# A weight conversion inside a mixture-of-experts kernel: its square one call later, its calls spread over the experts in another way

## The chip, the cores and the metric

The kernel runs on one core of a Trainium2 chip. Its time is device time in microseconds (us) of one execution; several runs are given by their median. A profile is one further execution, recorded by the hardware. Engines are called PE (TensorE, matmuls), DVE (VectorE), ACT (ScalarE), POOL (GpSimd) and SP (SyncE, which issues most DMAs).

## What is computed

Attention over 2304 tokens gives x (512 wide). Each token goes to two of eight experts, and a dense layer follows; the last two steps are

```python
top2 = np.argpartition(-noisy_logits, 2, axis=1)[:, :2]
h = np.maximum(x[mask] @ w1[e], 0.0)                  # 512 -> 1024, per expert e
out[mask] += top2_w[mask, k, None] * (h @ w2[e])      # 1024 -> 512
h = x @ w_in                                          # 512 -> 2048
g = np.maximum(0.01 * h, h)
return (g @ w_out).astype(np.float32)                 # 2048 -> 512
```

`w_in` and `w_out` come from random numbers divided by a square root, so they are 64-bit floats. The kernel gets their raw bits and turns them into 32-bit floats itself.

## The kernel before

**Stages.** Attention and routing come first, then the eight experts, then the dense layer. An expert has 640 rows of tokens (5 blocks of 128). A float32 matmul is made of three: every operand is kept as a rounded "high" half, written by ACT, and a "low" half (the difference, written by DVE).

**One expert.** `hidden(e, f)` (PE line 742) runs for f = 0 to 7: 24 matmuls into the PSUM tile ph, of which there are two; ACT writes the high half of hT (line 751), DVE the low half (752). Then, for each block k = 0 to 4: `transposed` turns the next expert's tokens (PE line 215 into the PSUM tile xtp, two of them; ACT 217 and DVE 218 write the halves of xT), and `expert_out(e, k)` runs 24 matmuls (line 763) into the PSUM tile py, two of them; ACT line 773 copies py out as ys, and SP stores that in y_d. `feed` loads weight chunks of later experts and splits them (ACT line 154, DVE 156).

**The conversion.** `narrow()` is the call that the change is about. 64 pieces of 128 x 256 numbers go through it as through a pipeline, one stage each per call. In the call that converts piece j: DVE lines 708, 711, 714 and 715 take the bits apart (715 is the last one that reads the low words), POOL line 718 adds, and ACT line 719 squares the high words into k, which lies in the place of the low words. In the next call, DVE line 689 compares k with a constant, which zeroes numbers that are too small. Pieces 0 to 31 (`w_out`) are then stored. Two pieces of `w_in` make one tile w8: POOL line 700 forms four sums from it, and two later calls split it (ACT line 670, DVE 672) and store it (SP lines 671, 675).

**Order.** In the expert stage ACT and DVE keep the order in which the program is written. The order of PE, POOL and SP is chosen when the kernel is built, by a scheduler with a model of the times; so an edit to ACT and DVE can also move matmuls.

**Where it is called.** In expert 0: 7 calls. In experts 1 to 6: at f = 0, 2, 4 and 6, and once after every block k, 9 calls. In expert 7: at every f, 8 calls. That is 69, as many as the 64 pieces and the stages behind them need. A loop after expert 7 would make up for calls that are missing.

Of the kernel before, what the change touches and what calls it, by code (L numbers as in the profile page):

```python
# [15 lines left out]
AF = mybir.ActivationFunctionType  # L16
# [12 lines left out]
E = 8  # L29
# [27 lines left out]
FH, FK, NF = 2, 2, 2  # L57
# [45 lines left out]
def body(ctx: ExitStack, tc, qT, kT, v, wgc, noise, eye, cst, w1, w2, win, wout, out):  # L103
    nc = tc.nc
# [53 lines left out]
    def feed(n, upto, pool=False):  # L158

        while loading:  # L160
            split_half(pool)
        for _ in range(n):
            if state["next"] < 2 * min(len(chunks), upto):
                c, h = divmod(state["next"], 2)
                state["next"] += 1
                raw = rawp.tile([P, 512], F32, tag="raw", name="raw")
                nc.sync.dma_start(raw, chunks[c][:, h * 512 : (h + 1) * 512])
                loading.append((c, h, raw))
# [33 lines left out]
    def gather(e, k):  # L202
        xg[e, k] = st.tile([P, DM], F32, tag="st", name="xg")
        i = k * E + e
        nc.gpsimd.indirect_dma_start(
            out=xg[e, k],
            out_offset=None,
            in_=x_d[0 : T1 * P if k < K1 else N, :],
            in_offset=bass.IndirectOffsetOnAxis(ap=gidx[:, i : i + 1], axis=0),
        )  # L210

    def transposed(src, dst, k):
        pt = b1.tile([P, 4, P], F32, tag="b1", name="xtp")
        for d in range(4):
            nc.tensor.transpose(pt[:, d, :], src[:, d * P : (d + 1) * P], ident)
        sl = slice(k * P, (k + 1) * P)
        nc.scalar.activation(dst[:, :, 0, sl], pt, AF.Copy)  # L217
        nc.vector.tensor_tensor(
            dst[:, :, 1, sl], pt, dst[:, :, 0, sl].bitcast(F32), op=ALU.subtract
        )  # L220
# [441 lines left out]
    loaded, converting, parted = [], [], []  # L662

    def narrow():

        if parted and parted[0][1] is not None:
            i, part, w8, x = parted[0]
            sl = slice(512 * x, 512 * x + 512)
            hi = cv.tile([P, 512], F32R, tag="hi", name="cvhi", bufs=1)
            nc.scalar.activation(hi, w8[:, sl], AF.Copy)  # L670
            nc.sync.dma_start(combos[i][:, part, 0, sl], hi.bitcast(F32))
            nc.vector.tensor_tensor(
                w8[:, sl].bitcast(F32R), w8[:, sl], hi.bitcast(F32), op=ALU.subtract
            )
            nc.sync.dma_start(combos[i][:, part, 1, sl], w8[:, sl])
            parted[0][3] += 1
            if x:
                parted.pop(0)
        if converting:
            c, part, k, mf = converting.pop(0)  # L680
            if c < 8:
                w = cv.tile([P, CV], F32, tag="w", name="cvw")
            else:
                if part % 2 == 0:
                    w8 = cv.tile([P, 1024], F32, tag="cvq", name="cvq")
                    parted.append([c - 8, None, w8, 0])
                w8 = parted[-1][2]
                w = w8[:, part % 2 * CV : (part % 2 + 1) * CV]
            nc.vector.scalar_tensor_tensor(w, k, SMALL, mf, op0=ALU.is_ge, op1=ALU.mult)
            if c < 8:  # L690
                nc.sync.dma_start(singles[c][:, part * CV : (part + 1) * CV], w)
            elif part % 2:
                q = lambda i: w8[:, i * P : (i + 1) * P]
                for d, x, y, op in (
                    (S1, A21, A22, ALU.add),
                    (S2, S1, A11, ALU.subtract),
                    (S3, A11, A21, ALU.subtract),
                    (S4, A12, S2, ALU.subtract),
                ):
                    nc.gpsimd.tensor_tensor(q(d), q(x), q(y), op=op)  # L700
                parted[-1][1] = part // 2
        if len(loaded) > 1 or loaded and state["narrowed"] == 16 * 1024 // CV:
            c, part, raw = loaded.pop(0)
            low, high = raw[:, :, 0], raw[:, :, 1]
            a = cv.tile([P, CV], I32, tag="a", name="cva", bufs=1)
            m = cv.tile([P, CV], I32, tag="m", name="cvm")
            mf, hf, k = m.bitcast(F32), high.bitcast(F32), low.bitcast(F32)
            nc.vector.tensor_scalar(
                a, high, 3, 0x3FFFFFF8, op0=ALU.logical_shift_left, op1=ALU.bitwise_and
            )  # L710
            nc.vector.scalar_tensor_tensor(
                a, high, -0x40000000, a, op0=ALU.bitwise_and, op1=ALU.bitwise_or
            )
            nc.vector.tensor_single_scalar(m, a, -0x800000, op=ALU.bitwise_and)
            nc.vector.scalar_tensor_tensor(  # L715
                mf, low.bitcast(U32), 2.0**-52, mf, op0=ALU.mult, op1=ALU.mult
            )
            nc.gpsimd.tensor_tensor(mf, mf, a.bitcast(F32), op=ALU.add)  # L718
            nc.scalar.activation(k, hf, AF.Square)  # L719
            converting.append((c, part, k, mf))  # L720
        i = state["narrowed"]
        if i < 16 * 1024 // CV:
            state["narrowed"] += 1
            c, part = divmod(i, 1024 // CV)
            raw = cv.tile([P, CV, 2], I32, tag="raw64", name="raw64", bufs=3)
            words = doubles[c].bitcast(I32).rearrange("p (n t) -> p n t", t=2)
            nc.sync.dma_start(raw, words[:, part * CV : (part + 1) * CV])
            loaded.append((c, part, raw))
# [3 lines left out]
    def hidden(e, f, n0=0, n1=CAP):  # L732

        parts = [(n0, n1)] if n1 - n0 <= 512 else [(0, 320), (320, 640)]
        m = parts[0][1] - parts[0][0]
        w = slot(8 * e + f // 2)
        ps = big.tile([P, 2, 512], F32, tag="big", name="ph")
        for d in range(4):
            col = d * 256 + (f % 2) * P
            for a, b in TERMS:  # L740
                for h, (m0, m1) in enumerate(parts):
                    nc.tensor.matmul(  # L742
                        ps[:, h, 0:m],
                        w[:, a, col : col + P],
                        xT[:, d, b, m0:m1],
                        start=(d == 0 and a == 0 and b == 0),
                        stop=(d == 3 and a == 1),
                    )
        src = ps[:, 0 : len(parts), 0:m]
        hv = hT[:, f, :, n0:n1].rearrange("p s (h n) -> p s h n", n=m)  # L750
        nc.scalar.activation(hv[:, 0], src, AF.Relu)  # L751
        nc.vector.scalar_tensor_tensor(  # L752
            hv[:, 1], src, 0.0, hv[:, 0].bitcast(F32), op0=ALU.max, op1=ALU.subtract
        )
# [22 lines left out]
    def expert_out(e, k):  # L777
        for _ in expert_parts(e, k):
            pass
# [144 lines left out]
    with tc.manual_schedule(engines=ORDERED0):  # L924
# [12 lines left out]
        for k in range(K1):  # L937
            for i, _ in enumerate(expert_parts(0, k)):
# [4 lines left out]
                if k == K1 - 1 and i >= TI and late:  # L943
                    gather_late()
                    e, j = late.pop(0)
# [9 lines left out]
    with tc.manual_schedule(engines=ORDERED):  # L955
        for f in range(8):
            hidden(0, f, K1 * P, CAP)
            feed(FH, (f + 1) // 2 + RING)
            if f % NF == 0:
                narrow()  # L960
            if f >= 8 - NB + K1:
                gather(1, f - 8 + NB)
    with tc.manual_schedule(engines=ORDERED):
        for k in range(NB):
            transposed(xg[1, k], xT, k)
        for k in range(K1, NB):
            expert_out(0, k)
            feed(FK, 4 + RING)
            narrow()
        for e in range(1, E):  # L970
            for f in range(8):
                hidden(e, f)
                feed(FH, 8 * e + (f + 1) // 2 + RING)
                if f % NF == 0 or e + 1 == E:
                    narrow()
                next(tokens, None)
                if f >= 3 and e + 1 < E:
                    gather(e + 1, f - 3)
            if e + 1 == E:
                break  # L980
            for k in range(NB):
                transposed(xg[e + 1, k], xT, k)
                expert_out(e, k)
                feed(FK, 8 * e + 4 + RING)
                narrow()
# [392 lines left out]
```

## Time and profile before

| | |
|---|---|
| median of 3 runs | 1010.89 us (1010.03 to 1013.91) |
| the profiled execution | 1014.06 us, its span 1012.3 us |
| PE busy | 960.9 us (95%), weight loads 862.7 us (85%) |
| DVE, ACT, POOL busy | 645.4 us, 376.1 us, 228.2 us |
| experts 1 to 7 | from about 186 us to about 607 us of the span |
| first and last of the 64 squares (line 719) | 174.9 us and 582.3 us |

Busy time is the time in which an engine executes. The view of the waits lists, for each pair of instructions, how long an engine sat idle in front of the first one, and which instruction ended that.

### The profile page before, as it was taken

The page shows a single profiled execution, that of the slowest core. Times are in us where ns is not written, and L with a number is a line of the kernel's source. Part 1 is how long each engine was busy: PE and PEld are TensorE (multiplying, and loading weights), DVE is VectorE, ACT ScalarE, POOL GpSimd, SP SyncE. Part 2 cuts the span into 40 slices and gives each one's busy share as a digit, 9 for nine tenths or more (in the row PEclk, how much of TensorE's full clock was granted, in tenths as well). Part 3 has the DMA queues.
Part 4 walks back from the last instruction along what each step waited for, and adds up shares of the span by engine and source line. Part 5 has one row for each costly group of instructions (what it writes and reads, how often), then busy time and mean ns, then how long its engine had stood idle before and what let it go on. Part 6 is the DMA issues. An engine that isn't in the chain of part 4 may idle for free. (4 is left out here: it accounts for less than half of the span.)

```text
span 1012.3 us, 15783 instructions
## 1 busy us (share of the span) xinstructions
PE 960.9 (95%) x5782; PEld 862.7 (85%) x5782; DVE 645.4 (64%) x1354; ACT 376.1 (37%) x729; POOL 228.2 (23%) x325
## 2 busy tenths in 40 slices
PE   6889879999999999999999998999999999999998
PEld 4788768998989899797897977989989988998897
DVE  5688855686775657766767833475566566556553
ACT  2644424443443434345353443332242232324112
POOL 2873452203122131422313222101001100000000
PEclk7889879999999999999999999999999999999999
DMA  9941346656465564866667586765646645645541
GB/s 267 323 156 62 101 143 194 219 175 210 147 192 164 187 185 157 264 202 222 213 207 224 201 285 229 257 247 207 230 171 210 244 168 200 222 148 193 213 146 42
DMA packets 85906, 198.09 MB, mean 196 GB/s; under 512 B 8960, under 2 KB 14528, under 8 KB 84672
## 3 DMA queue, kind: packets, MB, share of 16 engines
q1 hardware_dynamic: 79744, 177.11, 51.9%
q0 software_dynamic: 6080, 19.93, 6.5%
q8 instruction: 46, 0.75, 0.3%
q14 instruction: 36, 0.29, 0.1%
HBM read 156.11 MB, written 40.89 MB: 195 GB/s over the span
## 5 line engine op out<-in xcount | busy, mean ns | idle before, releaser
L1280 PE MATMUL po<-whB,gT 128*128 128x512 f32 x864 | 203.9, 392 | 0.0
L1280 PEld LDWEIGHTS po<-whB,gT 128*128 128x128 f32 x864 | 159.8, 188 | 31.9
L1244 PEld LDWEIGHTS pp<-zB,whA 128*128 128x128 f32 x1344 | 165.4, 192 | 6.9 <-ACT tmp L1252 3.5
L1244 PE MATMUL pp<-zB,whA 128*128 128x256 f32 x1344 | 167.7, 283 | 3.1 <-ACT tmp L1252 2.7
L763 PE MATMUL py<-whB,hT 128*128 128x512 f32 x600 | 148.8, 395 | 2.5 <-ACT ys L773 2.1
L742 PE MATMUL ph<-xT,whB 128*128 128x320 f32 x960 | 146.9, 309 | 2.4 <-ACT xT L217 2.4
L742 PEld LDWEIGHTS ph<-xT,whB 128*128 128x128 f32 x960 | 143.1, 188 | 5.8 <-ACT xT L217 3.1
L763 PEld LDWEIGHTS py<-whB,hT 128*128 128x128 f32 x600 | 109.6, 188 | 24.7 <-ACT ys L773 3.6
L1225 DVE TENSOR_TENSOR tmp<-tmp,pp 128x256 f32<-128x256 f32 x160 | 65.2, 418 | 65.5 <-PE pp L1244 61.6
L752 DVE SCALAR_TENSOR_TENSOR hT<-ph,hT 128x640 fp32r<-128x640 f32 (+2 forms) x72 | 53.9, 749 | 77.2 <-ACT hT L751 77.1
L742 PE MATMUL ph<-xT,whA 128*128 128x320 f32 (+2 forms) x576 | 94.2, 322 | 6.3 <-DVE hT L752 3.8
L742 PEld LDWEIGHTS ph<-xT,whA 128*128 128x128 f32 x576 | 90.2, 200 | 9.2 <-DVE hT L752 4.0
L763 PE MATMUL py<-whA,hT 128*128 128x512 f32 x360 | 89.3, 395 | 3.7 <-ACT ys L773 2.7
L1233 ACT ACTIVATE gT<-tmp 128x512 fp32r<-128x512 f32 x64 | 40.5, 632 | 134.5 <-DVE tmp L1230 134.5
L719 ACT ACTIVATE raw<-raw 128x256 f32<-128x256 f32 x64 | 28.1, 438 | 163.9 <-DVE cvm L715 132.7
L895 POOL DMA_INDIRECT g<-y_d,rows x36 | 34.0, 945 | 242.3 <-DVE g L906 167.8
L763 PEld LDWEIGHTS py<-whA,hT 128*128 128x128 f32 x360 | 65.6, 188 | 18.8 <-ACT ys L773 4.3
L718 POOL TENSOR_TENSOR cvm<-cvm,cva 128x256 f32<-128x256 f32 x64 | 48.0, 750 | 138.0 <-DVE cvm L715 120.8
L1234 DVE TENSOR_TENSOR gT<-tmp,gT 128x512 fp32r<-128x512 f32 x64 | 44.3, 692 | 46.3 <-ACT gT L1233 46.3
L751 ACT ACTIVATE hT<-ph 128x640 fp32r<-128x640 f32 (+2 forms) x72 | 45.9, 638 | 64.6 <-PE ph L742 64.6
L156 DVE TENSOR_TENSOR whB<-raw,whB 128x512 fp32r<-128x512 f32 x89 | 58.7, 688 | 10.5 <-ACT whB L154 10.3
L154 ACT ACTIVATE whB<-raw 128x512 fp32r<-128x512 f32 x96 | 57.2, 624 | 12.7 <-DMA raw<-in_w 8.3
(192 smaller groups left out, 1144.8 us busy)
## 6 DMA issues: line engine op xcount, KB each, us to landing
whA<-ws SPq DMA_DIRECT2D x64, 896.0 KB
raw<-in_w SPq DMA_DIRECT2D x128, 256.0 KB
y_d<-ys SPq DMA_DIRECT2D x40, 256.0 KB
raw<-in_wout SPq DMA_DIRECT2D x32, 256.0 KB
raw<-in_win SPq DMA_DIRECT2D x32, 256.0 KB
ws<-cvhi SPq DMA_DIRECT2D x32, 256.0 KB
ws<-cvq SPq DMA_DIRECT2D x32, 256.0 KB
whA<-ws SPq DMA_DIRECT2D x10, 512.0 KB
```

The source lines that it names most:

```text
L154: nc.scalar.activation(s[:, 0, sl], raw, AF.Copy)
L156: eng.tensor_tensor(s[:, 1, sl], raw, s[:, 0, sl].bitcast(F32), op=ALU.subtract)
L718: nc.gpsimd.tensor_tensor(mf, mf, a.bitcast(F32), op=ALU.add)
L742: nc.tensor.matmul(ps[:, h, 0:m], w[:, a, col : col + P], xT[:, d, b, m0:m1], start=(d == 0 and a == 0 and b == 0), stop=(d == 3 and a == 1),)
L751: nc.scalar.activation(hv[:, 0], src, AF.Relu)
L752: nc.vector.scalar_tensor_tensor(hv[:, 1], src, 0.0, hv[:, 0].bitcast(F32), op0=ALU.max, op1=ALU.subtract)
L763: nc.tensor.matmul(ps, hT[:, f, a, sl], w[:, b, col : col + DM], start=(f == 0 and a == 0 and b == 0), stop=(f == 7 and a == 1),)
L1225: add = lambda o, x, y: nc.vector.tensor_tensor(o, x, y, op=ALU.add)
L1233: nc.scalar.activation(gT[:, h, 0], ch(h), AF.Copy)
L1234: nc.vector.tensor_tensor(gT[:, h, 1], ch(h), gT[:, h, 0].bitcast(F32), op=ALU.subtract)
L1244: nc.tensor.matmul(out_, w[:, part, a, q * P : (q + 1) * P], zT["B"][:, j, part, b], start=(part == 0 and a == 0 and b == 0), stop=(part = ...
L1280: nc.tensor.matmul(sums[t], gT[:, h, a, sl], w[:, b, h * DM : (h + 1) * DM], start=(fp + h + a + b == 0), stop=(fp == 7 and h == 1 and a = ...
```

## The change

In `narrow()` the square moves from the call that takes a piece apart to the call after it, in front of the comparison that uses it and behind the split of the tile before. And the calls are spread differently: experts 1 to 6 get one more call, at f = 5 (10 instead of 9), and expert 7 has calls at f = 0, 2, 4 and 6 (4 instead of 8), 71 in all.

```diff
         if converting:
-            c, part, k, mf = converting.pop(0)
+            c, part, k, hf, mf = converting.pop(0)
+            nc.scalar.activation(k, hf, AF.Square)
             if c < 8:
...
             nc.gpsimd.tensor_tensor(mf, mf, a.bitcast(F32), op=ALU.add)
-            nc.scalar.activation(k, hf, AF.Square)
-            converting.append((c, part, k, mf))
+            converting.append((c, part, k, hf, mf))
...
             for f in range(8):
                 hidden(e, f)
                 feed(FH, 8 * e + (f + 1) // 2 + RING)
-                if f % NF == 0 or e + 1 == E:
+                if f % 2 == 0 or f == 5 and e + 1 < E:
                     narrow()
```

Three places show what moves. In the changed kernel the lines of the conversion have numbers one higher (715 is 716, 689 is 690), and the square is line 681.

**First place:** ACT and DVE in expert 5, from one block of tokens (k = 2) to the next. raw64 is a piece's tile of raw words, with the number of the piece's tile. ACT before:

```order
L217 ACTIVATE xT_109<-xtp_4961 128x4x128
L773 ACTIVATE ys_4993<-py_4968 128x512
L670 ACTIVATE cvhi_4996<-cvq_4894 128x512
L719 ACTIVATE raw64_4904<-raw64_4904 128x256
L217 ACTIVATE xT_109<-xtp_5013 128x4x128
```

DVE before, in the same stretch:

```order
L218 TENSOR_TENSOR xT_109<-xtp_4961,xT_109 128x4x128
L672 TENSOR_TENSOR cvq_4894<-cvq_4894,cvhi_4996 128x512
L689 SCALAR_TENSOR_TENSOR cvq_5001<-raw64_4809,cvm_4952 128x256
L708 TENSOR_SCALAR cva_5003<-raw64_4904 128x256
L711 SCALAR_TENSOR_TENSOR cva_5003<-raw64_4904,cva_5003 128x256
L714 TENSOR_SCALAR cvm_5004<-cva_5003 128x256
L715 SCALAR_TENSOR_TENSOR cvm_5004<-raw64_4904,cvm_5004 128x256
L218 TENSOR_TENSOR xT_109<-xtp_5013,xT_109 128x4x128
```

ACT's square is on tile 4904, which DVE takes apart in this very stretch; line 715 stands between. ACT in the changed kernel:

```order
L217 ACTIVATE xT_109<-xtp_5051 128x4x128
L773 ACTIVATE ys_5083<-py_5058 128x512
L670 ACTIVATE cvhi_5086<-cvq_4890 128x512
L681 ACTIVATE raw64_4899<-raw64_4899 128x256
L217 ACTIVATE xT_109<-xtp_5106 128x4x128
```

DVE in the changed kernel, in the same stretch:

```order
L218 TENSOR_TENSOR xT_109<-xtp_5051,xT_109 128x4x128
L672 TENSOR_TENSOR cvq_4890<-cvq_4890,cvhi_5086 128x512
L690 SCALAR_TENSOR_TENSOR cvq_5040<-raw64_4899,cvm_5043 128x256
L709 TENSOR_SCALAR cva_5097<-raw64_4997 128x256
L712 SCALAR_TENSOR_TENSOR cva_5097<-raw64_4997,cva_5097 128x256
L715 TENSOR_SCALAR cvm_5098<-cva_5097 128x256
L716 SCALAR_TENSOR_TENSOR cvm_5098<-raw64_4997,cvm_5098 128x256
L218 TENSOR_TENSOR xT_109<-xtp_5106,xT_109 128x4x128
```

The square is now on the tile that was taken apart a call earlier (4899), and DVE compares that tile (line 690) right behind it; the piece that DVE now takes apart (4997) is squared in the next call.

**Second place:** PE from the end of expert 5's hidden layer to the start of expert 6's. Of the groups of transposes (line 215) the last in each list is expert 7's, the others are expert 6's blocks 2 to 4. Before:

```order
L742 MATMUL ph<-xT,whB 128x320 x24
L763 MATMUL py<-whB,hT 128x512 x16
L215 MATMUL xtp<-ident,xg 128x128 x4
L763 MATMUL py<-whB,hT 128x512 x43
L215 MATMUL xtp<-ident,xg 128x128 x4
L763 MATMUL py<-whB,hT 128x512 x5
L742 MATMUL ph<-xT,whA 128x320 x2
L763 MATMUL py<-whB,hT 128x512 x13
L215 MATMUL xtp<-ident,xg 128x128 x4
L763 MATMUL py<-whB,hT 128x512 x11
L215 MATMUL xtp<-ident,xg 128x128 x4
L742 MATMUL ph<-xT,whA 128x320 x46
```

and in the changed kernel:

```order
L742 MATMUL ph<-xT,whB 128x320 x48
L763 MATMUL py<-whB,hT 128x512 x9
L742 MATMUL ph<-xT,whB 128x320 x24
L763 MATMUL py<-whB,hT 128x512 x23
L215 MATMUL xtp<-ident,xg 128x128 x4
L763 MATMUL py<-whB,hT 128x512 x41
L215 MATMUL xtp<-ident,xg 128x128 x4
L763 MATMUL py<-whB,hT 128x512 x11
L215 MATMUL xtp<-ident,xg 128x128 x4
L763 MATMUL py<-whB,hT 128x512 x20
L742 MATMUL ph<-xT,whA 128x320 x6
L215 MATMUL xtp<-ident,xg 128x128 x4
L742 MATMUL ph<-xT,whA 128x320 x42
```

The transpose of expert 6's last block, which had 11 matmuls of line 763 behind it before the hidden layer went on, now has 20. Behind f = 7, the last 24 matmuls of line 742, stand 23 of line 763 instead of 16.

**Third place:** PE from expert 0 to expert 1. Before:

```order
L763 MATMUL py<-whB,hT 128x512 x8
L742 MATMUL ph<-xT,whB 128x320
L215 MATMUL xtp<-ident,xg 128x128 x4
L763 MATMUL py<-whB,hT 128x512 x4
L215 MATMUL xtp<-ident,xg 128x128 x4
L763 MATMUL py<-whB,hT 128x512 x2
L742 MATMUL ph<-xT,whB 128x320 x23
L763 MATMUL py<-whB,hT 128x512 x24
```

and in the changed kernel:

```order
L763 MATMUL py<-whB,hT 128x512 x15
L742 MATMUL ph<-xT,whB 128x320 x2
L215 MATMUL xtp<-ident,xg 128x128 x8
L742 MATMUL ph<-xT,whB 128x320 x4
L763 MATMUL py<-whB,hT 128x512 x24
L742 MATMUL ph<-xT,whB 128x320 x42
```

The last transpose of expert 1's tokens had six matmuls of line 763 and another transpose behind it; now it has the transpose alone, and the matmuls that need its result follow at once.

## Rows read from the trace of the kernel before

**Rows 1.** The page's head and its busy times: engine, us, share of span, instructions.

```profile
span 1012.3 us, 15783 instructions
PE 960.9 (95%) x5782; PEld 862.7 (85%) x5782; DVE 645.4 (64%) x1354; ACT 376.1 (37%) x729; POOL 228.2 (23%) x325
```

**Rows 2.** Stretches: from:to, length, busy us (instructions) per engine, PE clock, DMA share, GB/s.

```profile
300.00:400.00 100.00, 99.98 (x589) 91.91 (x588) 60.39 (x124) 39.26 (x73) 22.22 (x28) 1.00 0.54 171
400.00:500.00 100.00, 94.96 (x525) 83.36 (x524) 70.72 (x138) 43.48 (x84) 35.34 (x56) 1.00 0.70 232
500.00:600.00 100.00, 94.66 (x528) 83.87 (x528) 71.20 (x133) 45.78 (x87) 24.40 (x42) 1.00 0.65 213
```

**Rows 3.** Waits, 170 to 600 us: who for whom, us in total, times, longest.

```profile
ACT raw L719 <- DVE cvm L715: 132.7, 48, 3.4
...
ACT whA L154 <- DMA raw<-in_w: 6.7, 7, 2.5
...
PE py L763 <- ACT ys L773: 4.8, 6, 1.6
...
PE ph L742 <- ACT xT L217: 3.7, 3, 1.4
...
PE py L763 <- ACT hT L751: 1.4, 3, 0.5
PE xtp L215 <- DVE xT L218: 1.3, 2, 1.0
```

**Rows 4.** PE in time, expert 5 to 6: start, us, instruction, count, [idle before].

```profile
484.52 0.60 PE L215 MATMUL xtp<-ident,xg 128*128 128x128 f32 x4
...
489.41 2.90 PE L742 MATMUL ph<-xT,whA 128*128 128x320 f32 x17 [1.33 <-ACT xT L217]
```

**Rows 5.** ACT in time, the same stretch.

```profile
484.25 0.59 ACT L773 ACTIVATE ys<-py 128x512 f32<-128x512 f32 x1
484.72 0.64 ACT L670 ACTIVATE cvhi<-cvq 128x512 fp32r<-128x512 f32 x1
488.44 0.43 ACT L719 ACTIVATE raw<-raw 128x256 f32<-128x256 f32 x1 [3.09 <-DVE cvm L715]
488.78 0.58 ACT L217 ACTIVATE xT<-xtp 128x512 fp32r<-128x512 f32 x1
```

**Rows 6.** DVE in time, the same stretch.

```profile
485.39 0.72 DVE L672 TENSOR_TENSOR cvq<-cvq,cvhi 128x512 fp32r<-128x512 f32 x1 [0.31 <-ACT cvhi L670]
...
487.78 0.63 DVE L715 SCALAR_TENSOR_TENSOR cvm<-raw,cvm 128x256 f32<-128x256 uint32 x1
489.39 0.69 DVE L218 TENSOR_TENSOR xT<-xtp,xT 128x512 fp32r<-128x512 f32 x1 [0.98 <-ACT xT L217]
```

**Rows 7.** DVE in time, hidden layer of expert 7, two calls in a row.

```profile
559.95 0.82 DVE L752 SCALAR_TENSOR_TENSOR hT<-ph,hT 128x640 fp32r<-128x640 f32 x1 [1.09 <-ACT hT L751]
...
564.24 0.64 DVE L715 SCALAR_TENSOR_TENSOR cvm<-raw,cvm 128x256 f32<-128x256 uint32 x1
565.97 0.82 DVE L752 SCALAR_TENSOR_TENSOR hT<-ph,hT 128x640 fp32r<-128x640 f32 x1 [1.09 <-ACT hT L751]
...
570.12 0.43 DVE L715 SCALAR_TENSOR_TENSOR cvm<-raw,cvm 128x256 f32<-128x256 uint32 x1
```

**Rows 8.** PE in time, hidden layer and outputs of expert 7.

```profile
558.33 3.68 PE L742 MATMUL ph<-xT,whB 128*128 128x320 f32 x24
...
593.16 14.39 PE L763 MATMUL py<-whA,hT 128*128 128x512 f32 x62 [1.62 <-ACT ys L773]
```

**Rows 9.** POOL in time, hidden layer of expert 7.

```profile
562.99 1.60 POOL L700 TENSOR_TENSOR cvq<-cvq 128x128 f32<-128x128 f32 x3 [3.31 <-DVE cvq L689]
564.96 0.74 POOL L718 TENSOR_TENSOR cvm<-cvm,cva 128x256 f32<-128x256 f32 x1 [0.36 <-DVE cvm L715]
```

**Rows 10.** ACT and DVE in time, expert 0 to expert 1.

```profile
184.69 0.62 ACT L217 ACTIVATE xT<-xtp 128x512 fp32r<-128x512 f32 x1
...
185.54 0.68 DVE L218 TENSOR_TENSOR xT<-xtp,xT 128x512 fp32r<-128x512 f32 x1
```

## The prediction

> **What bounds the kernel now.** The head of the page and its busy times come first: a span of 1012.3 us of which PE is busy 960.9 us [rows 1]. A gain must come out of the 51 us in which PE stands still, unless PE's work itself changes, and here it does not. The view by stretches then says where the change can act. The first piece is squared at 174.9 us and the last at 582.3 us, so experts 1 to 7 are the place. From 300 to 400 us PE is busy for 99.98 of 100 us, from 400 to 500 for 94.96 and from 500 to 600 for 94.66 [rows 2]. PE's clock is 1.00 in all three. So 5.0 + 5.3 = 10.4 us of idle PE lie where the pieces of `w_in` are split and stored besides being converted.
>
> The view of the waits from 170 to 600 us names who ends that idle time. PE waits 14 times: 4.8 us for ys, 3.7 for the high half of xT, 1.4 for hT, 1.3 for the low half of xT, 11.2 us together [rows 3]. All but the last are ACT's, and far above them in that view stands ACT itself: 132.7 us, 48 times, in front of the square (line 719), until DVE's line 715 is done [rows 3]. That costs nothing by itself, since ACT has time to spare. It costs something where PE wants an ACT instruction that stands behind the square.
>
> The three engines in order of time, at the start of expert 6, show one such case. PE transposes the last block at 484.52 us [rows 4]. ACT could copy it at once; but it has begun the split at 484.72, then waits 3.09 us for line 715, squares at 488.44, and copies the block at 488.78 [rows 5]. DVE ends line 715 at 487.78 + 0.63 = 488.41, writes the low half at 489.39 [rows 6], and PE's hidden layer starts at 489.41 after 1.33 us of waiting [rows 4]. The other waits that I followed, in experts 5 and 7, have the same pattern: a square just ahead on ACT, or DVE behind an ACT that was held up. The longest, 1.62 us, is in expert 7 [rows 8].
>
> **The change, part by part.** *The square a call later.* Its operand has then been ready for a whole call, so ACT no longer waits in front of it. Removed from PE's path: up to 11.2 us [rows 3]. The square still takes its 0.43 us of ACT [rows 5], 64 times, beside PE's work, as before.
>
> *The wait that is added.* DVE's comparison (690) now needs a square that stands behind ys and the split on the same ACT. Queued behind it on DVE are the four steps on the next piece and the low half of the next block, for which PE waits. From the start of ys to the end of that low half: ys to split 484.72 - 484.25 = 0.47 us, split to its subtraction 485.39 - 484.72 = 0.67 [rows 5, 6], from there to the end of line 715 488.41 - 485.39 = 3.02, the low half 0.69 [rows 6]; together 4.85 us. The square, 0.43 us, runs beside the subtraction of 0.72, so it adds nothing. ys of block 3 starts when PE has ended that block, and PE has the 24 matmuls of block 4 before the hidden layer of the next expert. At 14.39 us for 62 [rows 8] these take 5.57 us. That covers 4.85 with 0.7 to spare; so I charge only 0.3 us at each of the four expert changes 3-4 to 6-7, the size of DVE's wait for the split today (0.31) [rows 6]: **1.2 us**. Bounds: 0, and 4 x 1.33 = 5.3 us if every change waits as today [rows 4].
>
> *PE's new order.* At the change to expert 6 the last transpose has 20 matmuls behind it instead of 11, so the block has 9 x 0.23 = 2.1 us more to arrive: that is what makes the 4.85 us above fit. At expert 0 to 1 it is the other way round. The matmuls that need the last block now follow one transpose (0.60 us [rows 4]) behind it, and the copies take 0.62 on ACT and 0.68 on DVE [rows 10]: 1.30 - 0.60 = **0.7 us** lost. Bounds: 0 if the copies start early, 1.3 if nothing overlaps.
>
> *One call more in experts 1 to 6, four fewer in expert 7.* The work of the 64 pieces is the same. A call with everything that DVE does for one f lasts 559.95 to 564.88 us, 4.93 us, or 565.97 to 570.55, 4.58 us [rows 7]. In the new order PE has, from the end of f = 4 to the end of f = 7, three times 24 matmuls of 3.68 us [rows 8] and 14 of line 763: 14.3 us. DVE, now with calls at f = 4, 5 and 6, needs 3 x 4.93 = 14.8 us at most. What is late by 0.5 us is covered by the matmuls behind f = 7, 23 of line 763, of which 6 at most need f = 7: 17 x 0.23 = 3.9 us. Cost 0; if that cover were gone, 0.5 us x 6 = 3 us. The extra call also issues two stores and a load on SP and adds to POOL (three sums are 1.60 us, the addition 0.74 [rows 9]); neither is waited for by PE directly, and both are idle most of the time (POOL 228 of 1012 us [rows 1]). In expert 7 the calls vanish from f = 1, 3, 5 and 7, and with them what held up its share of the 11.2 us; nothing is counted twice.
>
> **Sum:** -11.2 + 1.2 + 0.7 = -9.3 us. The profiled execution took 1014.06 us, so it would take 1004.8. It lies 3.2 us above the median of the three runs, 1010.89; from the median the same sum gives **1001.6 us**.
>
> The Trainium skill, Perfetto Trace Analysis, section Identifying the Most-Contended Engine, says that matmul busy time misjudges how near TensorE is to its limit, and that the busy share of weight loads is the better measure. Here weight loads fall from 91.91 us in a stretch of 100 to 83.36 and 83.87 [rows 2], 16.6 us short where matmuls are 10.4 us short. By that measure the sum would be 6.2 us better, -15.5. I go by the idle time, because it is what can be filled, and the stretches differ in their mix of instructions.
>
> **Rivals.** *A. The wait changes sides.* PE gets rid of its waits for ys and hT, but DVE now arrives late with xT, since the comparison holds it up behind ys. For it: the margin is only 0.7 us, and PE's order was made by a model of times, not by this trace. Against it: 9 more matmuls of cover. Then the waits for xT, 3.7 + 1.3 = 5.0 us [rows 3], stay: -9.3 + 5.0 = -4.3, 1006.6 us.
>
> *B. DVE overruns at f = 4, 5 and 6, because loads come late.* Each f splits two loaded halves, ACT first, in front of the square and the next hT. Where a load was late, ACT waited up to 2.5 us [rows 3]. If each of the three calls is held up by that, one lasts 4.93 + 2.5 = 7.43 us; late at the end by 3 x 7.43 - 14.3 = 8.0, less the cover of 3.9: 4.1 us in each of six experts, 24.6 us. The result is 1010.9 - 9.3 + 24.6 = 1026.2. It turns slower by more than 0.5% (5.05 us) when an expert loses over 2.4 us, that is from 6.9 us per call. For it: SP has more to issue just there. Against it: such waits came 7 times in all for this tile, 6.7 us together [rows 3].
>
> *C. POOL holds DVE.* POOL's sums and its addition fall beside DVE's steps. If DVE stood still for them, a call would last 4.58 + 1.60 + 0.74 = 6.92 us [rows 7, 9], an expert would lose 3 x 6.92 - 14.3 - 3.9 = 2.6 us, and the three experts with sums in them (4 to 6) 7.7: -1.6, 1009.3 us. Against it: line 715 takes 0.64 us in a call with three sums and 0.43 in one without [rows 7], so DVE loses tenths. The Trainium skill, SBUF — State Buffer, section Who interferes with whom, says that a DVE instruction with two SBUF inputs and a GpSimd instruction that reads SBUF exclude each other, and the loser stands fully still; by that, C would be the rule. The trace does not agree: 0.2 us where 1.60 would be due.
>
> **How the numbers follow.** About 0.5%, 5.05 us, is what a measurement of this kernel can tell from no change. The forecast, a gain between 5 and 12 us, gets 0.64: the pattern is the same wherever I followed a wait, and the covers were worked out with the long call. A gets 0.26, C 0.04, B 0.06. So faster 0.64, same 0.26 + 0.04 = 0.30, slower 0.06. The range: its low end is the gain without any new loss, 11.2, and 1.2 us more for the spread of runs (the lowest of three lies 0.9 below their median), 998.5. Its high end takes in A and most of C, 1009.0. Left out are B, the bad end of A and C, and a gain above all bounds, some 0.18.
>
> **What would show it.** Right: ACT's wait for line 716 in front of the square (now 681) gone from the waits, or nearly; PE's waits for ys, hT and xT from 170 to 600 us down from 11.2 to about 2 us; PE busy over 98 of 100 us in the two stretches behind 400 us; a wait below 1.3 us at the change to expert 1. A shows as PE waiting for DVE xT at the expert changes, with DVE waiting for the square. B shows as PE waiting for hT (line 752) behind f = 7, and ACT for raw. C shows as DVE's steps of 1 us and more beside POOL's. I am wrong if PE's idle time between 170 and 600 us is still over 7 us, or if a wait of the same size appears behind 600 us, where the fetches of the token pairs start and I expect no change.

## The result and the profile after

The changed kernel took 999.71 us, median of four runs (997.6 to 1002.17), against 1011.45 us for four runs of the kernel before. The ratio is 0.9882, with a 95% interval of 0.9852 to 0.9912: between 15.0 and 8.9 us were gained, 11.7 in the middle. The forecast was 1001.6 us, in a range of 998.5 to 1009.0.

The head and the busy times of the page after, as in [rows 1]:

```profile
span 995.8 us, 15826 instructions
PE 954.7 (96%) x5782; PEld 860.4 (86%) x5782; DVE 645.4 (65%) x1354; ACT 376.8 (38%) x729; POOL 229.8 (23%) x325
```

PE ran the same 5782 matmuls. The span is 16.5 us shorter than the one before, which is more than the change did. The next rows show why: in both kernels, the first matmul of the experts (line 742) and the first of the dense layer (line 1182). Before:

```profile
115.59 0.39 PE L742 MATMUL ph<-xT,whA 128*128 128x256 f32 x1 [0.69 <-ACT xT L217]
...
612.88 0.39 PE L1182 MATMUL ph<-early,wi 128*128 128x256 f32 x1 [0.69 <-ACT early L217]
```

After:

```profile
112.10 0.38 PE L742 MATMUL ph<-xT,whA 128*128 128x256 f32 x1 [0.69 <-ACT xT L217]
...
596.48 0.39 PE L1182 MATMUL ph<-early,wi 128*128 128x256 f32 x1 [0.69 <-ACT early L217]
```

The experts began 3.5 us earlier in this one execution, before anything that the change touches; over all profiles of this study that start lies between 111.2 and 118.4 us. What the change did is in the stage between the two rows: 497.3 us before, 484.4 after, **12.9 us shorter**. From line 1182 to the last matmul it is 395.6 us in both. This length of the expert stage is used below for every kernel. One profile is one execution: two profiles of the changed kernel gave 484.4 and 483.7. The beginning of the stage, up to the first matmul of expert 1 (line 742, 128x320), takes 65 to 69 us in these profiles, and the mean granted clock from 120 to 150 us lies between 0.80 and 0.94. Where a few us of the stage are compared, the rest of it is therefore given too, called "from expert 1 on": 416.0 and 417.5 us in the two profiles of the changed kernel.

The three stretches of [rows 2], after:

```profile
300.00:400.00 100.00, 99.98 (x591) 92.34 (x590) 69.18 (x139) 41.11 (x77) 27.39 (x38) 1.00 0.61 188
400.00:500.00 100.00, 98.33 (x558) 88.47 (x557) 77.20 (x150) 47.94 (x91) 38.45 (x60) 1.00 0.78 253
500.00:600.00 100.00, 98.22 (x546) 87.34 (x545) 53.12 (x95) 41.60 (x76) 18.48 (x29) 1.00 0.63 212
```

From 400 to 600 us PE's idle time fell from 10.4 to 1.67 + 1.78 = 3.45 us, at the same clock of 1.00. From the view of the waits from 170 to 600 us, after (who for whom, us in total, times, longest):

```profile
...
ACT cvhi L670 <- DMA ws<-cvhi: 18.9, 10, 3.8
ACT whB L154 <- DMA raw<-in_w: 13.0, 11, 2.9
...
ACT whA L154 <- DMA raw<-in_w: 5.5, 4, 2.3
DVE cvq L690 <- ACT raw L681: 5.2, 2, 3.2
...
DVE cvw L690 <- ACT raw L681: 4.5, 2, 3.0
...
ACT raw L681 <- DVE cvm L716: 3.0, 3, 1.8
```

ACT's wait in front of the square is down from 132.7 us to 3.0. The wait that the change adds, DVE's comparison (690) for the square (681), is 5.2 + 4.5 = 9.7 us, but only four times. ACT's split (670) now waits 18.9 us, where it was 1.5, for the store of the tile before to leave cvhi, of which there is one buffer. The same view for PE alone, 170 to 620 us:

```profile
...
PE py L763 <- ACT ys L773: 1.4, 3, 0.5
PE xtp L215 <- DVE xT L218: 1.2, 2, 0.9
...
PE ph L742 <- DVE xT L218: 0.6, 1, 0.6
...
PE ph L742 <- issue: 0.3, 1, 0.3
```

The other three rows of this view are of line 1182, the dense layer, and the kernel before has them too. In the experts 1.4 + 1.2 + 0.6 + 0.3 = 3.5 us are left of 11.2 [rows 3]. The second profile of the changed kernel (e8, below) has 5.1 us, and there the low half of xT counts for more:

```profile
PE xtp L215 <- DVE xT L218: 2.1, 3, 1.6
...
PE ph L742 <- DVE xT L218: 1.3, 1, 1.3
```

**Where the change from expert 5 to 6 went.** PE, ACT and DVE in time, after, the place of [rows 4 to 6]:

```profile
474.12 0.60 PE L215 MATMUL xtp<-ident,xg 128*128 128x128 f32 x4
474.47 4.81 PE L763 MATMUL py<-whB,hT 128*128 128x512 f32 x20
479.12 1.04 PE L742 MATMUL ph<-xT,whA 128*128 128x320 f32 x6
480.00 0.60 PE L215 MATMUL xtp<-ident,xg 128*128 128x128 f32 x4
481.23 4.96 PE L742 MATMUL ph<-xT,whA 128*128 128x320 f32 x32 [0.62 <-DVE xT L218]
```

```profile
474.07 0.58 ACT L773 ACTIVATE ys<-py 128x512 f32<-128x512 f32 x1
475.81 0.64 ACT L670 ACTIVATE cvhi<-cvq 128x512 fp32r<-128x512 f32 x1 [1.16 <-DVE cvm L715]
476.35 0.43 ACT L681 ACTIVATE raw<-raw 128x256 f32<-128x256 f32 x1
476.68 0.58 ACT L217 ACTIVATE xT<-xtp 128x512 fp32r<-128x512 f32 x1
```

```profile
477.79 0.69 DVE L672 TENSOR_TENSOR cvq<-cvq,cvhi 128x512 fp32r<-128x512 f32 x1 [0.90 <-POOL cvq L701]
...
480.49 0.68 DVE L218 TENSOR_TENSOR xT<-xtp,xT 128x512 fp32r<-128x512 f32 x1
```

ACT squares 0.54 us behind the start of the split (476.35 - 475.81), where it took 3.72 before (488.44 - 484.72 [rows 5]). PE still stops, for 0.62 us instead of 1.33. The releaser is now DVE's low half, which stands behind the split's subtraction and the four steps on the next piece. In the second profile PE stops for 1.31 us at this place.

The transposes that wait (1.2 us) have another cause behind DVE. PE and ACT in time, after, one of them:

```profile
403.13 0.66 PE L215 MATMUL xtp<-ident,xg 128*128 128x128 f32 x4 [0.94 <-DVE xT L218]
```

```profile
401.11 0.63 ACT L154 ACTIVATE whB<-raw 128x512 fp32r<-128x512 f32 x1 [2.90 <-DMA raw<-in_w]
```

ACT waited 2.90 us for a load of weights and copied the block for DVE only then. The second of these transposes (0.29 us) stands behind a wait of 2.25 us of the same kind, and the longest in the second profile (1.59 us) behind one of 3.05.

### The profile page after: what moved, and what is told of

Read it like the earlier page. It is cut to its first block, busy times and chain, and to the rows that moved or that the text cites. A ratio compares the mean times of both kernels' runs of the same rounds, so it can differ in the third digit from the quotient of the medians.

```text
span 995.8 us, 15826 instructions
## 1 busy us (share of the span) xinstructions
PE 954.7 (96%) x5782; PEld 860.4 (86%) x5782; DVE 645.4 (65%) x1354; ACT 376.8 (38%) x729; POOL 229.8 (23%) x325
## 5 line engine op out<-in xcount | busy, mean ns | idle before, releaser
L763 PE MATMUL py<-whA,hT 128*128 128x512 f32 x360 | 87.3, 393 | 0.9 <-ACT ys L773 0.9
L156 DVE TENSOR_TENSOR whB<-raw,whB 128x512 fp32r<-128x512 f32 x89 | 60.1, 704 | 12.9 <-ACT whB L154 12.9
L205 POOL DMA_INDIRECT xg<-x_d,gidx x40 | 40.9, 1021 | 67.8 <-PE xtp L215 53.9
```

The lines of the kernel that those rows point to most:

```text
L156: eng.tensor_tensor(s[:, 1, sl], raw, s[:, 0, sl].bitcast(F32), op=ALU.subtract)
L763: nc.tensor.matmul(ps, hT[:, f, a, sl], w[:, b, col : col + DM], start=(f == 0 and a == 0 and b == 0), stop=(f == 7 and a == 1),)
```

## The experiments

The kernels of one batch ran on one chip beside the kernel before: 1010.79, 1010.12 and 1011.54 us in the three batches. With each run stands the length of its expert stage (497.3 us before).

**Which half of the change does it.** Four kernels. The first (e1) moves the square and keeps the old calls.

```diff
-                if f % 2 == 0 or f == 5 and e + 1 < E:
+                if f % NF == 0 or e + 1 == E:
```

> The square a call later, the calls as before (f = 0, 2, 4, 6 in experts 1 to 6, every f in expert 7). Theory M (PE's stops came from ACT being held in front of the square): nearly the whole gain is here, 1000 to 1003 us, and ACT's wait for line 716 in front of the square, 132.7 us before, is under 10 us. Rival S (the gain came from taking calls out of expert 7): 1009 to 1012 us, as before.

Measured: 1000.27 us, ratio 0.9895 (0.9863 to 0.9927), stage 482.6 us (416.4 from expert 1 on). From its waits:

```profile
ACT raw L681 <- DVE cvm L716: 2.8, 3, 1.8
...
PE xtp L215 <- DVE g L906: 2.6, 1, 2.6
```

The gain is there without the spread, as theory M has it and against S. It is not the gain of the wait alone: with the square's place the order of PE has changed too, and at the change from expert 5 to 6 the last transpose has 21 matmuls of line 763 behind it, as many as in e3 below, where the kernel before has 11. The one larger wait that is left (2.6 us, DVE's line 906 late) lies behind expert 7, which has eight calls here, where the changed kernel has four.

The second (e2) has the new calls and the square in its old place.

```diff
-            c, part, k, hf, mf = converting.pop(0)
-            nc.scalar.activation(k, hf, AF.Square)
+            c, part, k, mf = converting.pop(0)
...
-            converting.append((c, part, k, hf, mf))
+            nc.scalar.activation(k, hf, AF.Square)
+            converting.append((c, part, k, mf))
```

> The square where it was, the calls spread as in the change. Theory M: only expert 7's stops go (0.50 + 0.48 + 1.62 us of idle time, some 3.5 us with what a stop costs beside it), and the call at f = 5 adds a hold-up of ACT of 3 us in six experts that PE's buffers mostly cover: 1007 to 1011 us, PE's waits for ys and xT in experts 4 to 6 still there. Rival S: 999 to 1002 us.

Measured: 1017.11 us, ratio 1.0063 (1.0041 to 1.0085), stage 500.9 us. It is slower than before, and above the 1007 to 1011 us that M allowed: a miss. PE and then ACT in time, expert 4:

```profile
409.49 1.67 PE L763 MATMUL py<-whA,hT 128*128 128x512 f32 x6 [1.33 <-ACT hT L751]
...
419.33 4.63 PE L763 MATMUL py<-whA,hT 128*128 128x512 f32 x19 [1.49 <-ACT ys L773]
```

```profile
408.42 0.43 ACT L719 ACTIVATE raw<-raw 128x256 f32<-128x256 f32 x1 [3.08 <-DVE cvm L715]
408.75 0.69 ACT L751 ACTIVATE hT<-ph 128x640 fp32r<-128x640 f32 x1
...
417.88 0.43 ACT L719 ACTIVATE raw<-raw 128x256 f32<-128x256 f32 x1 [3.14 <-DVE cvm L715]
...
418.69 0.59 ACT L773 ACTIVATE ys<-py 128x512 f32<-128x512 f32 x1
```

ACT stands 3.08 us in front of the square, then writes hT, for which PE has waited. Stops like these come again in experts 5 and 6. With ACT held in each call, three calls in a row at f = 4, 5 and 6 do not fit under PE's matmuls: the mechanism of rival B, with ACT's wait for line 715 where B had a late load. PE's order at these changes is still the old one, with 11 matmuls behind the last transpose. So the spread by itself costs some 6 us by the medians (the interval allows 4 to 9) and 3.6 by the stage, and is free only once the square's wait is gone.

The third (e3) leaves the square in its old place and the old calls, but gives it a tile of its own, so that it need not wait for line 715 to read the low words. (w8 became a view of w16, to make room.)

```diff
-            mf, hf, k = m.bitcast(F32), high.bitcast(F32), low.bitcast(F32)
+            mf, hf = m.bitcast(F32), high.bitcast(F32)
+            k = cv.tile([P, CV], F32, tag="k", name="cvk")
```

> The kernel before, with the square written to a tile of its own instead of over the low words, so that it stays in its call but no longer waits for line 715 (two scratch tiles of the token rows share memory to make room). Theory M, which says that the wait counts and not the place: as the square alone, 1000 to 1003 us. Rival P (the place counts, or having the square and its comparison in one call): 1009 to 1012 us.

Measured: 1001.95 us, ratio 0.9903 (0.9867 to 0.9939), stage 484.7 us (417.7 from expert 1 on). PE's busy time from 200 to 580 us, in this kernel:

```profile
200.00:580.00 380.00, 379.26 (x2176) 344.87 (x2174) 275.86 (x573) 167.07 (x316) 100.61 (x147) 1.00 0.64 203
```

The same stretch has 370.78 us before and 376.64 after. The place of the square in the program is not what counts. Theory P falls. What is shown to count is that the square has no wait, together with the order of PE that the scheduler then builds; no kernel here has PE's new order with ACT still held as before.

The fourth (e4) takes the changed kernel and gives cvhi a second buffer.

```diff
-            hi = cv.tile([P, 512], F32R, tag="hi", name="cvhi", bufs=1)
+            hi = cv.tile([P, 512], F32R, tag="hi", name="cvhi", bufs=2)
```

> The changed kernel with two buffers for cvhi instead of one (the same two scratch tiles share memory). In the changed kernel ACT waits 18.9 us, 10 times, for the store of cvhi to land before line 670. Theory W (these waits are behind what is left of PE's stops in experts 3 to 6, 0.94 + 0.62 + 0.29 us of idle time): 1 to 2.5 us below the changed kernel, 997 to 999 us, the waits gone. Rival H (they are hidden, the stops come from DVE's load): within 0.5 us of the changed kernel, and PE's waits for xT stay.

Measured: 997.92 us, ratio 0.9867 (0.9833 to 0.9902), stage 485.4 us. From its waits:

```profile
ACT raw L681 <- DVE cvm L716: 15.0, 10, 3.4
...
ACT cvhi L670 <- DMA ws<-cvhi: 1.5, 1, 1.5
```

The wait for the store is gone (18.9 to 1.5 us), and the one in front of the square has come back in its place, 3.0 to 15.0. The stage is no shorter (416.5 from expert 1 on), and PE's waits for the low half of xT are still there, 2.4 us: rival H by the profile. The time lies where W had it, but does not tell this kernel from the changed one. ACT, no longer held at the split, reaches the square before the tile that it overwrites is read. So the new wait is not shown to cost time.

**Is ACT's work the price, or its wait?** The changed kernel again, in the second batch (e8):

> The changed kernel once more, as the base for the three runs beside it on the same chip: a ratio of 0.985 to 0.991 to the kernel before, by every theory. If the ratio lies over 0.992, part of the first result was the chip or the run.

Measured: 997.05 us, ratio 0.9847 (0.9809 to 0.9884), stage 483.7 us, just below the range given. Beside it, the changed kernel with every square done twice, the second on the same operands as the first (e5):

```diff
+            nc.scalar.activation(k, hf, AF.Square)
             nc.scalar.activation(k, hf, AF.Square)
```

> The changed kernel with every square done twice: 64 x 0.43 = 27.5 us more work on ACT, but no new wait. Theory M (what cost PE time was ACT held up, not ACT's work): within 1.5 us of the changed kernel, PE's waits for ys, hT and xT up by 1 us at most. Rival L (ACT's load counts): 3 us or more above it, with PE waiting for ACT in experts 4 to 6.

Measured: 999.54 us, ratio 0.9879 (0.9839 to 0.9919), stage 484.2 us. From 200 to 580 us, the changed kernel and then this one (PE, PEld, DVE, ACT, POOL):

```profile
200.00:580.00 380.00, 375.62 (x2158) 341.56 (x2157) 276.29 (x572) 167.34 (x315) 99.87 (x146) 1.00 0.64 205
```

```profile
200.00:580.00 380.00, 375.81 (x2153) 341.37 (x2152) 276.10 (x570) 192.80 (x373) 99.62 (x145) 1.00 0.64 205
```

ACT works 25.5 us more and PE is as busy as in the changed kernel. The median is 2.5 us higher, more than the 1.5 that M allowed and less than the 3 of L, but the intervals overlap, and from expert 1 on it is 417.4 us against 417.5. So of those 25.5 us little or nothing is shown to reach the time. ACT's work on the square is not the price.

**Both ways of taking waits away.** The changed kernel with two buffers of cvhi, and with a tile of its own for the moved square (e6):

```diff
+            k = cv.tile([P, CV], F32, tag="k", name="cvk", bufs=1)
             nc.scalar.activation(k, hf, AF.Square)
```

> The changed kernel with two buffers for cvhi and the square in a tile of its own (one buffer; scratch tiles of the token rows share memory), so that ACT waits neither for the store of cvhi nor for line 716 of the call before (15.0 us, 10 times, in the run with two cvhi). Theory W (what is left of PE's stops comes from these two): PE's waits for xT, 2.4 us with two cvhi, go under 0.7 us, and the time is 1 to 3 us below the changed kernel. Rival H (they come from DVE's own load of ten calls per expert): PE's waits for xT stay at 1 to 2.5 us, and the time is within 1 us of the changed kernel.

Measured: 1003.46 us, ratio 0.9929 (0.9901 to 0.9956), stage 488.7 us (423.0 from expert 1 on): **slower** than the changed kernel beside it, which neither theory had. And the same with the old calls (e7):

> As the run beside it, but with the calls as in the kernel before (9 in experts 1 to 6, 8 in expert 7). Theory W: with nothing left that holds ACT up, the spread of the calls matters little: within 1.5 us of the run beside it, PE without waits for xT in experts 1 to 6, and 1 to 3 us of waits after expert 7, where the calls now delay the first token pairs. Rival H: DVE's lighter experts make it 1 us or more faster than the run beside it.

Measured: 1001.15 us, ratio 0.9893 (0.9857 to 0.9929), stage 487.8 us; PE is busy for 378.48 of 380 us from 200 to 580, so what it lacks against e1 lies before and behind that stretch. By its median it is 2.3 us faster than e6, as rival H has it and more than the 1.5 that W allowed, but the intervals overlap. PE's waits for xT in experts 1 to 6 are gone but for one of 0.25 us.

The waits of e6 point at the loads of the weights (line 154 splits them); the second view is of SP's queue:

```profile
ACT whB L154 <- DMA raw<-in_w: 28.6, 19, 3.9
...
ACT whA L154 <- DMA raw<-in_w: 14.3, 7, 3.5
```

```profile
SPq L728 <- ACT cvk L682: 41.7, 15, 4.4
```

PE's order is that of the changed kernel, instruction by instruction; SP's is not. With a tile of its own for k, a raw tile comes free with the square instead of with the comparison, so the scheduler put the loads of raw words (line 728) elsewhere, ahead of loads of weights (line 167). There SP waits for the square. The next batch tests that as theory Q: first by the tile of its own alone, with one cvhi as in the changed kernel (e10).

> The changed kernel with the square in a tile of its own, one buffer of cvhi. PE's and POOL's order is that of the changed kernel; SP's order is, but for some rows, that of the slow run with both tiles, where ACT waited 42.9 us for loads of weights at line 154 instead of 18.5. Theory Q (that run was slow because SP's order puts loads of the next piece, which must wait for ACT and DVE, in front of loads of weights): slow as that run, 1001 to 1005 us, with over 30 us of such waits. Rival R (it was slow because of the second cvhi, or the shared scratch tiles): as the changed kernel, 997 to 1000 us, or a gain.

Measured: 1007.65 us, ratio 0.9955 (0.9926 to 0.9985), stage 488.3 us (422.0 from expert 1 on). The loss is there with the tile alone, as Q has it, with 41.0 us of waits for loads of weights, though the time is above the 1001 to 1005 us that Q gave. SP, ACT and PE in time, expert 3, show the loss at one place:

```profile
345.21 0.33 SPq L728 DMA_DIRECT2D raw<-in_wout  x1
345.63 0.86 SPq L167 DMA_DIRECT2D raw<-in_w  x2
```

```profile
344.77 0.42 ACT L682 ACTIVATE cvk<-raw 128x256 f32<-128x256 f32 x1
...
349.50 0.63 ACT L154 ACTIVATE whA<-raw 128x512 fp32r<-128x512 f32 x1 [3.20 <-DMA raw<-in_w]
350.04 0.58 ACT L217 ACTIVATE xT<-xtp 128x512 fp32r<-128x512 f32 x1
```

```profile
351.51 0.66 PE L215 MATMUL xtp<-ident,xg 128*128 128x128 f32 x4 [1.60 <-DVE xT L218]
```

SP issues the raw load right behind the square's end (344.77 + 0.42 = 345.19), and the load of weights only after it. ACT waits 3.20 us for those weights, copies the block late, and PE stands for 1.60 us. The load that is needed follows 0.42 us behind the raw load, so it is not shown to have waited for anything else; the one that was held is the raw load in front of it. To show it the other way round, SP's order was fixed to that of the program in the expert stage, first in e6 (e11; PE's order differs from that of e6 in 4 of the stage's 2685 places):

```diff
-    with tc.manual_schedule(engines=ORDERED):
+    with tc.manual_schedule(engines=ORDERED | {mybir.EngineType.SP}):
```

> The run with both tiles, with SP too in the order in which the program is written for the experts. Theory Q: the loss against the changed kernel goes, 996 to 1000 us, and ACT's waits for loads of weights fall below 25 us. Rival R: it stays at 1001 to 1005 us.

Measured: 997.75 us, ratio 0.9859 (0.9825 to 0.9893), stage 479.3 us (413.6 from expert 1 on). Its waits for weights:

```profile
ACT whB L154 <- DMA raw<-in_w: 7.5, 15, 1.1
...
ACT whA L154 <- DMA raw<-in_w: 4.4, 10, 0.9
```

The loss is gone: 28.6 + 14.3 us of waiting became 11.9. Then the same line in the changed kernel, without the extra tiles (e12):

> The changed kernel with SP in the order in which the program is written; against the run beside it, it differs only by the two tiles, with one order on PE, POOL and SP. Theory Q: within 2 us of the changed kernel, and the two tiles are worth 0 to 2 us in the run beside it. If SP's written order is bad by itself, both are slow, above 1002 us, and the pair still tells the price of the tiles.

Measured: 996.82 us, ratio 0.9849 (0.9814 to 0.9884), stage 479.5 us (414.1 from expert 1 on). So the tiles are worth nothing (479.3 against 479.5). Against 484.4 and 483.7 the order of SP looks like 4 to 5 us of stage, but part of that is its beginning: from expert 1 on it is 414.1 against 416.0 and 417.5, 2 to 3.4 us. By time it could not be told from the changed kernel, whose ratio of the second batch is 0.9847.

**Does the call at f = 5 make DVE late?** The last kernel (e9) takes the call at f = 5 from experts 4 to 6 and gives experts 1 to 3 one at f = 3.

```diff
-                if f % 2 == 0 or f == 5 and e + 1 < E:
+                if f % 2 == 0 or f in (3, 5) and e < 4:
```

> The changed kernel with the additional calls in experts 1 to 3 (at f = 3 and 5), where the pieces are not yet split and stored, and none at f = 5 of experts 4 to 6; expert 7 as in the change. PE's idle time from 200 to 580 us was 3.4 us in the changed kernel and 1.1 us with the old calls. Theory D (what is left of PE's stops comes from the ten heavy calls in experts 4 to 6): PE's waits for xT in experts 4 to 6 fall below 0.7 us, no wait of 2 us behind expert 7, and the time is 0 to 3 us below the changed kernel. Rival E (more calls cost the same wherever they stand): the stops move to experts 1 to 3, and the time is that of the changed kernel within 1.5 us.

Measured: 997.51 us, ratio 0.985 (0.9813 to 0.9886), stage 481.7 us (415.1 from expert 1 on). PE no longer waits for xT inside experts 4 to 6; of the waits for DVE this is left, behind expert 7:

```profile
PE xtp L215 <- DVE g L906: 0.9, 1, 0.9
```

That is what theory D asked of the profile, for 1 to 2.4 us from expert 1 on; the time doesn't separate it. But it does not show that DVE's load was the cause: with the calls, ACT's waits for loads of weights went as well, from 18.5 and 21.6 us in the changed kernel to 4.8. And e12, which keeps all ten calls and only has SP in another order, has a single wait for the low half of xT, 0.4 us. More than half of what D put on DVE, 1.2 of 1.8 us and 1.9 of 3.4 in the two profiles, stood behind late loads. Three kernels (e9, e11, e12) thus beat the kernel before by about 1.5%. None is shown to beat the changed one.

## Why the prediction was right, point by point

**The bound and the cause: right, with one share open.** The gain came out of PE's idle time, and what had to end was ACT held in front of the square. e1 and e3, two different ways of ending that wait, give 1.05% and 0.97% without the spread. In the trace of before, nine of the 14 waits, 7.4 us together, are for an ACT instruction that stands right behind a square, or one copy further, and ACT had waited 2.8 to 3.4 us in front of that square, longer than any of the nine. But PE's new order came with the edit in e1 and e3 too, and its 2.1 us more of cover at a change of experts would by themselves be more than the stops there (0.97, 1.33 and 1.44 us). How much of the 12 us the order would give with ACT still held was not tried; nearest comes e4, where ACT is held 10 times for 15.0 us under the new order and the stage is no longer for it.

**"The same pattern" wherever a wait was followed: not so for the longest.** Before the 1.62 us in expert 7 [rows 8] there is no square: the last one is at 582.3 us, and ACT's split (670) at 591.99 us had waited 0.69 us for the store of cvhi. In two more waits for ys, 0.46 us each in experts 1 and 2, nothing held ACT; it had been waiting for PE itself, and the changed kernel still has them.

**The -11.2 us of waits removed: too much by 2.6.** The three waits for ys that are left (1.4 us, the longest 0.5) and the two before a transpose (1.2 us) were counted as gone. With what the prediction charged for new waits (1.2 + 0.7), 1.9 us were to remain; 3.5 did, and 5.1 in the second profile.

**The 4 x 0.3 us at the expert changes.** One of the four showed, with 0.62 us, and with 1.31 in the second profile, as much as the 1.33 of before. The chain from ys to the low half was put at 4.85 us under a cover of 5.57. It took from 474.07 to 481.17, 7.10 us: the split waited 1.16 us on top, its subtraction 0.90 for one of POOL's sums (line 701). The cover with its six matmuls of line 742 is what kept that to 0.62. Rival A's mechanism was at work here, at an eighth of its price in the first profile, 0.62 of 5.0 us, and at a quarter in the second. The transposes that waited for DVE, 1.2 and 2.1 us, stand for the most part behind late loads of weights, a term that the sum did not have.

**The 0.7 us from expert 0 to 1.** Measured 0.3, and put down to the issue.

**The extra call, costed at nothing: right, on a condition that was not named.** It is free because ACT is not held any more; without that it costs some 6 us (e2). The rows that it was worked out from show the condition: the long call is 4.93 us, but the next one begins 565.97 - 559.95 = 6.02 us after it [rows 7], because DVE stood 1.09 us for an ACT that was held. Three times 6.02 is 18.1 us, 3.8 more than the 14.3, and the cover was 3.9. That the spread gains something of its own is not shown: from expert 1 on it is 416.4 us without it and 416.0 and 417.5 with it, and the ratios 0.9895, 0.9882 and 0.9847 agree within their intervals.

**The size: right for a reason that was partly missing.** By idle time alone the sum would be short: 11.2 - 3.5 = 7.7 us, and 1.0 more from two waits of a transpose for line 906, 0.76 and 0.27 us behind 600 us in the trace of before, where the prediction expected no change; the view above has none of them. The rest of the 12.9 us of the stage is a term that the sum did not have. **A stop of PE costs more than the idle time shown.** The group of 20 matmuls above is shown with 4.81 us, yet the next group starts 4.65 us after it; the four transposes at 474.12 with 0.60, and the next starts after 0.35. The matmuls overlap in these rows, and a stop takes that overlap away. The transposes at 480.00 are followed at 481.23: 1.23 us against 0.35, so the stop cost 0.88 us where 0.62 are shown. Counted over every start of a matmul from 186 to 640 us against the usual distance of its kind, the stops cost 21.0 us before (14.8 of it shown as idle) and 8.9 after (5.8 shown): 12.1 us gained, of which 9.0 are shown. That is an estimate, which hangs on which start counts as late: counted only where a gap of over 0.15 us is shown, it is 18.0 and 7.3, a gain of 10.7. It stands beside 12.9 of the stage and 11.7 of the median.

So the number came out well partly by luck: the sum took too much off the idle time, and left out what a stop costs beside it.

The prediction gave a measure that sees this: by the Trainium skill, Perfetto Trace Analysis, section Identifying the Most-Contended Engine, the busy share of weight loads says more of TensorE than that of matmuls. In the two stretches behind 400 us weight loads rose by 8.6 us and busy matmuls by 6.9, so the rule agrees in direction. As a forecast it went too far: it gave 15.5 us, as if all 16.6 us of the shortfall could be had, and 11.53 + 12.66 - 2 x 7.66 = 8.9 us of shortfall are still there, measured against the stretch from 300 to 400 us of the trace after. The stage gained 12.9, between the two sums.

**The rivals.** B did not happen in the change as it was drawn, behind f = 7, though loads came late there too (18.5 us of ACT's waits). Its overrun came in e2, by ACT's wait, and in e6 and e10 PE waited once for the low half of hT, 0.65 and 0.43 us, behind loads for which ACT had stood 3.77 and 3.56 us. C did not: line 716 takes 0.42 to 0.67 us in the expert stage, and DVE waited for one of POOL's sums twice, 1.8 us together, once at the place above. The 1.60 us that the prediction sets against C's 0.2 us are three sums of 0.46 to 0.53 us [rows 9], so 1.60 for one DVE step was never due, and the 0.2 us say less against the two engines shutting each other out than the prediction has it. The doubt that the order of PE was made by a model of times was sound, but it was SP's order that mattered. What PE's new order is worth alone stays open.

## What to carry to other kernels

An engine that waits costs nothing by itself: ending 132.7 us of it, with the order of PE that followed, was worth 12; look for what stands behind the waiting instruction on the same engine, and whether the bottleneck needs that. Count a stop of the bottleneck by the distance between starts, not by the gap that a view shows. When an edit to one engine lets a scheduler reorder another, compare the orders before a gain is put down to the edit alone. And when a buffer's last reader changes, look at the queue that refills it: in e10 a load that waited there held up the loads of weights behind it.

## What the hardware showed beyond that

A tile more made the kernel slower. The own tile for the square, meant to free a wait, took the changed kernel from 0.9882 and 0.9847 to 0.9955 of the time before; with SP's order fixed, two tiles more cost nothing (e11 and e12). And 25.5 us more of work on ACT, in the same batch of runs as the changed kernel, moved PE's busy time from 200 to 580 us by 0.2 us. DVE's line 715 takes 0.42 to 0.43 us in 47 of its 62 runs from 186 to 600 us before, and 0.63 to 0.64 in the 15 that overlap one of POOL's sums in time.
